# Reordered copies, transposes and output products in the attention stages of a four-layer kernel

## The chip, the cores and the metric

The kernel runs on one core of one Trainium2 chip. The metric is the device time of one execution in microseconds (us). All times below come from the runs of the kernel before the change and from one profiled execution of it.

## The reference, cut to what matters

Four layers run one after the other on one array `x` of 2048 positions by 512 channels (bf16). The first and third layers are a long convolution ("A"), the second and fourth a dilated local attention ("B"). Every layer works on a normalised copy of `x` and adds its result back:

```python
x = A_u
x = x + _A_ref(_layernorm(x), ...)      # convolution by FFT over 4096 points, per channel
x = x + _B_ref(_layernorm(x), wqkv, wo) # attention, 32 heads of 16, 8 taps at distance 2
x = x + _A_ref(_layernorm(x), ...)      # the same weights again
x = x + _B_ref(_layernorm(x), wqkv, wo)

def _B_ref(x, wqkv, wo):                # H = 32, Dh = 16, W = 8, dil = 2
    q, k, v = split_heads(x @ wqkv)
    idx = pos[:, None] - 2 * arange(8)[None, :]
    attn = softmax(where(idx >= 0, einsum(q, k[idx]) / 4, -1e9))
    return einsum(attn, v[idx]) @ wo
```

## The kernel before, in words

The kernel keeps `x` in one tile `X` of 128 partitions by 16 columns of 512 channels; `slot(m)` says which column the m-th block sits in. The change is about the two B layers. Both are built by `b_layer`; the first runs with `ln_next` (it prepares the normalisation of the A layer that follows), the second with `store` (it writes the output).

**Steps.** A B layer has N = 36 steps t. Step t takes two blocks of 114 queries out of 72 (two parities of the sequence, two halves of the heads, two quarters in each half, nine blocks). Its work on the engines is:
- `logits(t)` (L1123, PE): 16 small products of keys `KS` and queries `QS` into `S`, a PSUM tile of four banks of which there is one; then the exponential on ACT into `PT` (L1126).
- `values(t - 2)` (L1142, PE): 16 products of `PT` and `V` into the bank `O`, of which there is one; then DVE takes the reciprocal of the sums (L1146) and writes the scaled values `on` (L1150).
- two to four units of `jobs` between them: `proj` (two units of two products, L1089; DVE copies the result to a stage tile `st`, L1094, and two DMAs on the SP queue scatter its even and odd rows into `KS` or `QS`, L1097), `vproj` (one unit, L1106), and `out` (two units of two products, L1177, then the addition to `X`). `jobs` are sorted by a due step, with a first step before which they may not run: 13 for the projections of the second parity, 24 for `out`.

**Order.** On PE, DVE, ACT, POOL and SP the instructions of a B layer stand in the order in which the Python code emits them (`tc.manual_schedule`). [...]

**Late columns.** Of the 16 columns of the normalised input, the first eight are turned on PE before step 0. The other eight are made while the steps run, by `late(t)`, in two groups g = 2 and 3 of four. Each group takes four emissions, at the steps named in `steps`: statistics (DVE) and the inverse deviation (`ln_den_b`, POOL, L225 and L226); scales (DVE, L230 and L231) and four normalised columns `xq` (POOL, L260); two DMA transposes `xt<-xq` on the SP queue (L1249); four copies of the turned data into `XU` (POOL, L1255). `XU` holds the transposed input `xnT` of all projections. Its second parity needs both groups, and is first read by the projections of step 13.

**Turned values.** Every three steps the values of three steps stand in one tile `on`. `turn_o(g)` issues a DMA transpose `oS<-on` on SP (L1158) and right behind it emits the copy `oT<-oS` on POOL (L1159). It is called at t = 4, 7, 10 and so on, ahead of `late(t)` in the same step. The last two groups of three are turned on PE instead (`turn_last`, L1169, copied by DVE at L1171).

**The tail.** `out(m)` for m below 8 uses the even columns and runs inside the steps. The products of m = 8 to 15 need the last values. `ahead(m, n)` begins two of them early with n dummy products (L1326); the rest run after the last values. An odd m of the second B layer gets its residual by a product with the identity (L1199) and leaves through ACT (L1200), all others through DVE (L1195, L1202, or L236 in the tail of the first B layer). In the first B layer ACT sums the squares of the eight last columns (L241, `square`), takes two roots (L247), and DVE, POOL and ACT write the normalised columns (`unorm`, L1186 and L1183) that the A layer begins with.

**Start.** `spread` (L1080) scatters two early projections, with two SP DMAs each; `fill(n)` emits n of the statistics in the list `left` (L212). The A layer interleaves its first products `s1` with the last normalisations, which it calls as `finish[1](0)` and `finish[1](1)` (L947 and L950).

Of the kernel before, what the change touches and what calls it, by code (L numbers as in the profile page):

```python
# [816 lines left out]
def a_layer(nc, tc, C, X, kt_dram, XU, ln_b, finish):  # L817

    with ExitStack() as es:
# [123 lines left out]
        with tc.manual_schedule(engines={mybir.EngineType.PE, mybir.EngineType.DVE, mybir.EngineType.Activation}):  # L943
            s1(0, on_dve)
            finish[0]()
            s1(1, on_act)
            finish[1](0)  # L947
            warm(2)
            s1(2, split=True)
            finish[1](1)  # L950
            warm(5)
            s1(3, split=True)
            warm(3)
            zpair(0)
            turn_pe(0)
            s1(4)
            s2(0, True)
            turns(2)
            turn_pe(1, (on_act, on_act))
            ahead = {0: (5, 6), 1: (7, 8)}  # L960
            for i in range(16):
                if 0 < i < 7:
                    s2(i)
                if 6 <= i < 15:
                    s2(i + 1)
                product(i)
                if 0 < i:
                    inverse(i - 1, i > 10)
                for k in ahead.get(i, (i + 7,)):
                    if k < 16:  # L970
                        s1(k, on_dve if k == 5 else on_act)
                if i in (1, 4, 8):
                    k = i // 4 * 4 + 4
                    turns(k)
                    turns(k + 2)
                if i >= 5:
                    final(i - 5, on_dve if i in (6, 8) else on_act)
                if 10 <= i < 14:
                    ln_b.gather(X, 0, 2 * i - 20, 2 * i - 18)
            final(11)  # L980
            ln_b.gather(X, 1, 0, 3)
            inverse(15)
            ln_b.gather(X, 1, 3, 8)
            ln_b.gather(X, 0, 8, 10)
            for k in range(12, 16):
                final(k)


def b_layer(nc, tc, C, X, Wt, ln_b, XU, left, store=None, ln_next=None):

    with ExitStack() as es:
# [84 lines left out]
        def spread(k, ps, eng):  # L1076
            T, t = sets[0][1 - k // 2 % 2], stp.tile([128, 512], BF, name="st", tag="st")
            eng(t[:], ps[:])
            for e in range(2):
                nc.sync.dma_start(T[e::2, e, k // 4, UF + 512:UF + 1024], t[e::2, :])  # L1080

        def proj(n, k, eng=on_dve):

# [44 lines left out]

        ons = {}

        def values(t):
            par, fp = t // NB // 2, t // NB % 2
            pt = PT[t % 3]
            for x in range(2):
                assert (par, fp, (t % NB * 2 + x) % NB) in ready, (t, x, done)
            O = psO.tile([128, 512], F32, name="O", tag="O")[:, 0:16 * DH + 16].rearrange("p (a b) -> p a b", b=DH + 1)
            for i in range(4):
                for sl in range(4):
                    x, e = sl // 2, sl % 2
                    f2, b = (t % NB * 2 + x) // NB, (t % NB * 2 + x) % NB  # L1140
                    c0 = (i * 4 + sl) * NQ
                    nc.tensor.matmul(O[:, x * 8 + i * 2 + e, :], pt[:, c0:c0 + 128],  # L1142
                                     V[:, par * NB + b, (fp * 2 + f2) * 8 + i * 2 + e, :], start=True, stop=True,
                                     skip_group_check=True)
# [5 lines left out]
            nc.vector.tensor_tensor(on.rearrange("q (h d) -> q h d", d=DH), O[:, :, 0:DH],  # L1150
                                    rd[:].unsqueeze(2).to_broadcast([128, 16, DH]), ALU.mult)
# [4 lines left out]
        def turn_o(g):  # L1156
            oS = ld.tile([128, 6, 128], BF, name="oS", tag="oS")
            nc.sync.dma_start_transpose(oS[:], ons[g][:])  # L1158
            nc.gpsimd.tensor_copy(turned_o(g // 3, g % 3 * 3).rearrange("f (b q) -> f b q", q=NQ), oS[:, :, 0:NQ])  # L1159

        pts = {}

        def turn_last(t):
            g, s = t // 3, t % 3
# [53 lines left out]
        with tc.manual_schedule(engines={mybir.EngineType.PE, mybir.EngineType.DVE, mybir.EngineType.Activation,  # L1218
# [14 lines left out]
            def late(t):  # L1233
                if t < 4:
                    fill((len(left) + 3 - t) // (4 - t))
                for g, steps in ((2, (1, 2, 4, 6)), (3, (4, 5, 7, 9))):
                    m0 = g * 4
                    if t == steps[0]:
                        assert not [j for p, j in left if j < m0 + 4]
# [20 lines left out]
                nc.scalar.activation(ln_b.den[:, js], ln_b.mv[:, js, 1], ACT.Sqrt, bias=ln_b.eps[:, 0:1])  # L1260
            last = len(ln_b.parts) - 1
            left = list(left)
            if ln_next is not None:
                fill(3)
            ln_b.gather(X, last, 0, 4)
            ln_b.aggregate(0, 4)
            root(0)
# [5 lines left out]
            ln_b.aggregate(4, 8)  # L1273
            root(1)
            pt0 = turned(xn)
            fill(2)
            ln_b.scales(4, 8)
            xn = normed(1, (2,), (3,))
            pre = sm.tile([128, 1], F32, name="pre", tag="pre")
# [19 lines left out]
            for n in range(4):  # L1299
# [1 line left out]
                for k in ((4, 6, 5, 7) if n == 0 else (0, 2, 1, 3, 4, 6, 5, 7)):  # L1301
                    jobs.append((NB * n + k // 4 * 4 + k % 2 * 2 - 3, 2, proj(n, k), 0 if n < 2 else 13))
                jobs += [(NB * n + b // 2 + 1 + b / 100, 1, vproj(p, n % 2, b), 0 if n < 2 else 13) for b in range(NB)]
            jobs += [(N - 9 + m, 2, out(m), 24) for m in range(8)]
            jobs.sort(key=lambda j: j[0])
            due = [(d, sum(j[1] for j in jobs if j[0] <= d)) for d, *_ in jobs]
            total = due[-1][1]
# [21 lines left out]
            for t in range(N):  # L1329
                need = max([c for d, c in due if int(d) <= t] + [0])  # L1330
                end = min(total, max(need, done + ((2, 4, 4, 4, 4)[t] if t < 5 else 3)))
                if t:
                    logits(t)
                work(end - 1, t)
                if 2 <= t < N - 1:
                    values(t - 2)
                work(end, t)
                if t == N - 1:
                    assert not jobs
                    values(N - 3)  # L1340
                    ahead(8, 1)
                    turn_last(N - 4)
                    values(N - 2)
                    ahead(9, 3)
                elif t == N - 3:
                    turn_last(t - 3)
                elif t == N - 2:
                    turn_last(t - 3)
                elif t >= 4 and t % 3 == 1:
                    turn_o(t // 3 - 1)  # L1350
                late(t)
            work(total, N)
            if ln_next is not None:
                ln_next.aggregate(0, 8, C["half"])
# [1 line left out]
            values(N - 1)  # L1356
            turn_last(N - 3)
            turn_last(N - 2)
            for m in (8, 9):
                omm(tail[m], m, (2,))  # L1360
            turn_last(N - 1)
            if ln_next is not None:
                ln_next.scales(0, 8)
                for m in range(8):
                    unorm(m, nc.gpsimd)
            psS = banks("b_psL", 4)
            for m in range(10, 14):
                tail[m] = sps([128, 512])[:]
            omm(tail[10], 10, (0, 1, 2))
# [30 lines left out]
def kernel(  # L1400
# [37 lines left out]
    finish = b_layer(nc, tc, C, X, Wt, ln_b, XU, [(0, j) for j in range(12, 16)] + [x for x in late if x[0] == 1], ln_next=ln)  # L1438
# [33 lines left out]
```

## Time and profile before

| what | value |
|---|---|
| median of 7 runs | 535.7 us (531.95 to 538.41) |
| the profiled execution's own time | 535.41 us |
| its span | 533.6 us |
| mean granted PE clock | 0.936 of full speed |
| busy PE / DVE / ACT / POOL | 395.0 / 434.4 / 350.6 / 79.8 us |
| first B layer: first to last exponential | 265.50 to 352.21 us |
| second B layer: first to last exponential | 432.29 to 519.31 us |

The profile's span lies 1.8 us below the time of the same execution; what is outside it is not seen by the engines. A row of the timeline gives start, duration, engine, line, operation and, in brackets, how long the engine sat idle before it and on what. One exponential is issued per step, so the distance from one row `PT<-S` to the next is the length of a step. A row of the windows view gives the stretch, its length, the busy time of each engine, the granted PE clock, and the DMA share.

### The profile page before, as it was taken

How to read it: one execution, taken by the hardware profiler on the slowest of the kernel's cores; microseconds unless marked ns; L12 is line 12 of the kernel's file. 1: busy time of each engine (PE TensorE's matmuls, PEld its weight loads, DVE VectorE, ACT ScalarE, POOL GpSimd, SP SyncE). 2: the span in 40 equal slices, each digit the busy share in tenths (PEclk: the TensorE clock that was granted, in tenths of full speed). 3: DMA queues.
4: the chain of work that ended last, by engine and by line, in shares of the span. 5: the costliest groups of instructions: out<-in, count | busy, mean ns of one | idle time of the engine just before them, and what ended most of it. 6: DMA issues, size and time to landing. Idle time of an engine off the chain costs nothing.

```text
span 533.6 us, 15408 instructions
## 1 busy us (share of the span) xinstructions
PE 395.0 (74%) x6534; PEld 254.5 (48%) x6534; DVE 434.4 (81%) x972; ACT 350.6 (66%) x422; POOL 79.8 (15%) x129
## 2 busy tenths in 40 slices
PE   0200466487568475699898899988899788989997
PEld 0100333256246443565565465655575555646664
DVE  4999999979998997978886467887899987656663
ACT  3999834446355553544777587868888676858872
POOL 0000000000000002051137401134000214621110
PEclk9999997869688877989999799999999999989999
DMA  8301057362563247803626423317685013533542
GB/s 264 139 1 39 1 110 99 73 129 71 119 72 128 68 95 139 211 10 120 209 84 129 96 80 88 51 18 188 133 192 80 2 41 90 119 88 76 111 90 81
DMA packets 105017, 52.52 MB, mean 98 GB/s; under 512 B 86003, under 2 KB 100724, under 8 KB 103668
## 3 DMA queue, kind: packets, MB, share of 16 engines
q1 hardware_dynamic: 103364, 51.14, 41.4%
q8 instruction: 51, 0.84, 0.7%
q10 hardware_dynamic: 1584, 0.39, 0.4%
q14 instruction: 18, 0.15, 0.1%
HBM read 17.96 MB, written 8.13 MB: 49 GB/s over the span
## 4 chain that ended last, share of the span: by engine, by line
PE 33%; DVE 27%; DMA 7%; ACT 6%; issue 3%; POOL 3%; SPq 2%; ACTq 0%; DVEq 0%; POOLq 0%
PE psG L1089 6%; PE psG L1106 4%; PE O L1142 4%; PE S L1123 4%; DMA zt<-Z 3%; DVE Ytab L656 3%; DVE Y2tab L658 3%; PE psG L1177 3%; ACT PT L1126 2%; DVE ln_st_b L212 2%; DVE ta L619 2%; DVE tb L620 2%; DMA oS<-on 2%; POOL XU L1255 2%; DMA xt<-xq 1%
## 5 line engine op out<-in xcount | busy, mean ns | idle before, releaser
L1126 ACT ACTIVATE PT<-S 128x1824 bf16<-128x1824 f32 x72 | 121.8, 1691 | 42.3 <-PE S L1123 42.0
L1089 PE MATMUL psG<-XU,wqk 128*128 128x512 bf16 x224 | 65.5, 396 | 3.9 <-POOL XU L1255 3.6
L1094 DVE CAST st<-psG 128x512 bf16<-128x512 f32 x56 | 38.5, 687 | 21.8 <-PE psG L1089 20.9
L1142 PEld LDWEIGHTS <-PT 128*128 128x128 bf16 x1152 | 39.2, 96 | 18.7 <-DVE on L1150 5.8
L1142 PE MATMUL O<-V,PT 128*128 128x17 bf16 x1152 | 40.2, 171 | 3.9 <-DVE on L1150 3.5
L307 PE MATMUL psA<-X,sb_F 128*128 128x128 bf16 x128 | 13.8, 242 | 36.4 <-ACT X L720 35.2
L1106 PE MATMUL psG<-wv,XU 128*128 128x256 bf16 x288 | 40.4, 273 | 0.2 <-DVE st L1094 0.2
L307 PEld LDWEIGHTS <-sb_F 128*128 128x128 bf16 x256 | 16.2, 102 | 44.1 <-issue 41.7
L1123 PEld LDWEIGHTS <-KS 32*128 32x128 bf16 x1152 | 20.3, 94 | 28.8 <-issue 23.2
L294 ACT CAST Z<-psA 128x1024 bf16<-128x1024 f32 (+1 forms) x32 | 28.8, 984 | 7.0 <-PE psA L307 7.0
L675 PE MATMUL psk<-Ytab,Xtab 128*32 128x64 bf16 x1024 | 23.9, 206 | 12.6 <-issue 6.9
L1150 DVE TENSOR_TENSOR on<-O,rd 128x256 bf16<-128x256 f32 x72 | 30.6, 425 | 2.5
L332 PE MATMUL psA<-zt,sb_C 128*128 128x512 bf16 x30 | 15.4, 539 | 22.9 <-DMA zt<-Z 22.9
L678 PE MATMUL psk<-Y2tab,Xtab 128*32 128x48 bf16 x1024 | 23.0, 202 | 11.6 <-issue 9.5
L1123 PE MATMUL S<-QS,KS 32*128 32x114 bf16 x1152 | 28.3, 213 | 4.1 <-DMA KS<-st 1.4
L656 DVE TENSOR_TENSOR Ytab<-Ytab,MA 128x2048 bf16<-128x2048 bf16 (+1 forms) x33 | 30.7, 930 | 0.2
L658 DVE TENSOR_TENSOR Y2tab<-Ytab,MB 128x2048 bf16<-128x2048 bf16 (+1 forms) x33 | 30.7, 929 | 0.0
L1146 DVE RECIPROCAL rd<-O 128x16 f32<-128x16 f32 x72 | 18.2, 253 | 14.6 <-PE O L1142 13.1
L684 ACT CAST KTq<-psk 128x1024 bf16<-128x1024 f32 (+1 forms) x9 | 8.3, 918 | 33.2 <-issue 32.6
L1159 POOL COPY oT<-oS 128x684 bf16<-128x684 bf16 x20 | 15.1, 757 | 99.4 <-DMA oS<-on 99.4
L633 POOL MEMSET Xtab<- 128x64 bf16 x8 | 1.5, 187 | 180.6 <-PE psk L678 133.6
L678 PEld LDWEIGHTS <-Xtab 128*32 128x32 bf16 x1024 | 20.6, 101 | 16.3 <-issue 15.4
(249 smaller groups left out, 1080.9 us busy)
## 6 DMA issues: line engine op xcount, KB each, us to landing
kt_scratch<-Kt SPq DMA_DIRECT2D x4, 1024.0 KB, 3.9
Kt<-kt_scratch SPq DMA_DIRECT2D x4, 1024.0 KB, 5.5
QS<-st SPq DMA_DIRECT2D x60, 64.0 KB, 1.9
KS<-st SPq DMA_DIRECT2D x60, 64.0 KB, 1.9
X<-in_A_u_dram SPq DMA_DIRECT2D x4, 512.0 KB, 5.1
out_dram<-X SPq DMA_DIRECT2D x16, 128.0 KB, 1.8
k_scratch<-KTq SPq DMA_DIRECT2D x7, 256.0 KB, 2.4
KT<-k_scratch SPq DMA_DIRECT2D x7, 256.0 KB, 2.8
```

The lines of the kernel that those rows point to most:

```text
L294: self.nc.scalar.copy(dst, src)
L307: nc.tensor.matmul(o, F1[:, j, r, :], rhs_j(j), start=True, stop=not dk)
L656: nc.vector.tensor_tensor(v(Y[:, :, :, q * EYB:(q + 1) * EYB, :]), src, vm(self.mult(self.MA, lev, hc, EYB)), ALU.mult)
L658: nc.vector.tensor_tensor(v(Y2[:, :, :, (q - 1) * EYB:q * EYB, :]), src, vm(self.mult(self.MB, lev, hc, EYB)), ALU.mult)
L678: nc.tensor.matmul(psk[32 * g:32 * g + 32, ds, EYB:], xs, Y2[:, 1 - m // 2, h, :, t], start=False, stop=(m == 3), skip_group_check=True)
L1089: nc.tensor.matmul(ps[:], wqk[:, ct, f0:f0 + 128], xnT[:, ct, par, UF + h * 512:UF + h * 512 + 512], start=(ct == 0), stop=(ct == 3))
L1094: eng(t[:], ps[:])
L1106: nc.tensor.matmul(ps[:].rearrange("p h d -> p (h d)"), xnT[:, ct, par, NQ * b + 1:NQ * b + 1 + NK], wv[:, ct, fp * 256:fp * 256 + 256], s ...
L1123: nc.tensor.matmul(S[:, i, sl * NQ:(sl + 1) * NQ], KS[r, e, f2, b * NQ + 1:b * NQ + 1 + NK], QS[r, e, f2, UF + b * NQ:UF + b * NQ + NQ], s ...
L1126: nc.scalar.activation(pt[:, 0:16 * NQ].rearrange("k (i x) -> k i x", i=4), S[:, :, 0:4 * NQ], ACT.Exp, scale=DH ** -0.5)
L1142: nc.tensor.matmul(O[:, x * 8 + i * 2 + e, :], pt[:, c0:c0 + 128], V[:, par * NB + b, (fp * 2 + f2) * 8 + i * 2 + e, :], start=True, stop= ...
L1150: nc.vector.tensor_tensor(on.rearrange("q (h d) -> q h d", d=DH), O[:, :, 0:DH], rd[:].unsqueeze(2).to_broadcast([128, 16, DH]), ALU.mult)
```

## The change

It is one patch of seven edits:
1. `place_o` is split from `turn_o`. The transpose of group g stays at t = 3g + 4; its copy into `oT` is emitted at t = 3g + 6. `late(t)` now comes ahead of both in the step.
2. Group 3 of the late columns issues its transposes at step 6 (was 7) and its copies at step 8 (was 9).
3. `spread` issues its odd rows (e = 1) on the POOL queue, its even rows on SP.
4. Three statistics (`fill(3)`) ahead of the last gather are left out in the first B layer, and the next fill emits one instead of two; the four go to steps 0 to 3. The list `left` of that layer is sorted by group.
5. `out` jobs have due steps 28 to 33 (were 27 to 34), and from t = 32 on a step runs all its units after `values`.
6. In the last step, `values(34)` takes a bank of the `psG` pool instead of `O`, and the early start of m = 9 with its three dummies is gone. The tail takes the products in the order 8, 10, 11, 9, 12 to 15, and three of them (10, 11, 12) are begun before the last turned group is there. The first root of the squares comes after m = 12 (was 11).
7. In the A layer, the last normalisations (`finish[1](1)`) are emitted ahead of `s1(2)`.

```diff
@@ a_layer
             finish[1](0)
             warm(2)
+            finish[1](1)
             s1(2, split=True)
-            finish[1](1)
             warm(5)
@@ spread
-            for e in range(2):
-                nc.sync.dma_start(T[e::2, e, k // 4, UF + 512:UF + 1024], t[e::2, :])
+            for e, q in ((1, nc.gpsimd), (0, nc.sync)):
+                q.dma_start(T[e::2, e, k // 4, UF + 512:UF + 1024], t[e::2, :])
@@ values
-            O = psO.tile([128, 512], F32, name="O", tag="O")[:, 0:16 * DH + 16].rearrange("p (a b) -> p a b", b=DH + 1)
+            O = (gps([128, 512]) if other else psO.tile([128, 512], F32, name="O", tag="O"))[:, 0:16 * DH + 16].rearrange("p (a b) -> p a b", b=DH + 1)
@@ turn_o
             oS = ld.tile([128, 6, 128], BF, name="oS", tag="oS")
             nc.sync.dma_start_transpose(oS[:], ons[g][:])
+            oSs[g] = oS
+
+        def place_o(g):
+            oS = oSs[g]
             nc.gpsimd.tensor_copy(turned_o(g // 3, g % 3 * 3).rearrange("f (b q) -> f b q", q=NQ), oS[:, :, 0:NQ])
@@ late
-                for g, steps in ((2, (1, 2, 4, 6)), (3, (4, 5, 7, 9))):
+                for g, steps in ((2, (1, 2, 4, 6)), (3, (4, 5, 6, 8))):
@@ start of the layer
-            if ln_next is not None:
-                fill(3)
...
-            fill(2)
+            fill(1 if ln_next is not None else 2)
@@ jobs
-            jobs += [(N - 9 + m, 2, out(m), 24) for m in range(8)]
+            jobs += [((28, 29, 30, 31, 32, 33, 33.5, 33.5)[m], 2, out(m), 24) for m in range(8)]
@@ the loop over t
                 if t:
                     logits(t)
-                work(end - 1, t)
+                if t < N - 4:
+                    work(end - 1, t)
                 if 2 <= t < N - 1:
                     values(t - 2)
                 work(end, t)
+                late(t)
                 if t == N - 1:
                     assert not jobs
                     values(N - 3)
+                    values(N - 2, True)
                     ahead(8, 1)
-                    turn_last(N - 4)
-                    values(N - 2)
-                    ahead(9, 3)
-                elif t == N - 3:
-                    turn_last(t - 3)
-                elif t == N - 2:
+                if t >= N - 3:
                     turn_last(t - 3)
                 elif t >= 4 and t % 3 == 1:
                     turn_o(t // 3 - 1)
-                late(t)
+                if t >= 6 and t % 3 == 0:
+                    place_o(t // 3 - 2)
@@ the tail
-            for m in (8, 9):
-                omm(tail[m], m, (2,))
+            omm(tail[8], 8, (2,))
+            psS = banks("b_psL", 4)
+            for m in range(10, 14):
+                tail[m] = sps([128, 512])[:]
+            omm(tail[10], 10, (0, 1, 2))
+            omm(tail[11], 11, (0, 1, 2))
             turn_last(N - 1)
+            omm(tail[12], 12, (0, 1, 2))
...
-            for m in range(8, 16):
-                if m > 13:
+            for m in (8, 10, 11, 9, 12, 13, 14, 15):
+                if m == 9:
+                    tail[m] = gps([128, 512])[:]
+                elif m > 13:
                     tail[m] = sps([128, 512])[:]
-                omm(tail[m], m, (3,) if m < 11 else (0, 1, 2, 3))
+                omm(tail[m], m, (3,) if m in (8, 10, 11, 12) else (0, 1, 2, 3))
                 odone(tail[m], m)
...
-                    if m == 11:
+                    if m == 12:
                         ln_next.root_sums(8, 12)
```

More of the change, by code (lines that the diff above doesn't have):

```diff
@@ L1129, in b_layer, with values @@
         ons = {}
-        def values(t):
+        def values(t, other=False):
             par, fp = t // NB // 2, t // NB % 2
@@ L1158, in turn_o @@
             nc.sync.dma_start_transpose(oS[:], ons[g][:])
+            oSs[g] = oS
+        def place_o(g):
+            oS = oSs[g]
             nc.gpsimd.tensor_copy(turned_o(g // 3, g % 3 * 3).rearrange("f (b q) -> f b q", q=NQ), oS[:, :, 0:NQ])
-        pts = {}
+        pts, oSs = {}, {}
         def turn_last(t):
@@ L1365, in b_layer @@
                     unorm(m, nc.gpsimd)
[L1366 to L1369, printed above, removed]
-            for m in range(8, 16):
-                if m > 13:
+            for m in (8, 10, 11, 9, 12, 13, 14, 15):
+                if m == 9:
+                    tail[m] = gps([128, 512])[:]
+                elif m > 13:
                     tail[m] = sps([128, 512])[:]
-                omm(tail[m], m, (3,) if m < 11 else (0, 1, 2, 3))
+                omm(tail[m], m, (3,) if m in (8, 10, 11, 12) else (0, 1, 2, 3))
                 odone(tail[m], m)
@@ L1437 @@
     late = [(p, j) for g in (2, 3) for p in range(3) for j in range(g * 4, g * 4 + 4)]
-    finish = b_layer(nc, tc, C, X, Wt, ln_b, XU, [(0, j) for j in range(12, 16)] + [x for x in late if x[0] == 1], ln_next=ln)
+    finish = b_layer(nc, tc, C, X, Wt, ln_b, XU, sorted([(0, j) for j in range(12, 16)] + [x for x in late if x[0] == 1], key=lambda x: x[1] // 4), ln_next=ln)
     a_layer(nc, tc, C, X, kt_dram, XU, ln_b2, finish)
```

## The prediction

> **What bounds the kernel now.** The page's table of groups comes first. It shows ACT waiting for `S` between exponentials, 42 us in all over 72 steps.
>
> ```profile
> L1126 ACT ACTIVATE PT<-S 128x1824 bf16<-128x1824 f32 x72 | 121.8, 1691 | 42.3 <-PE S L1123 42.0
> ```
>
> Next the timeline, filtered to ACT, for the length of each step. There is one `S`: logits follow the exponential that frees it. A smooth step is therefore 1.69 (exponential) + 0.49 (logits) + 0.05 = 2.23 us. Three units of PE work fit beneath it (two projection units 0.86, one vproj 0.45, values 0.43, logits 0.31: 2.05); four units give 2.5 to 2.6. Three steps of the first B layer are far longer, those that begin t = 7, 13 and 14:
>
> ```profile
> 282.07 1.69 ACT L1126 ACTIVATE PT<-S 128x1824 bf16<-128x1824 f32 x1 [0.54 <-PE S L1123]
> 285.69 1.69 ACT L1126 ACTIVATE PT<-S 128x1824 bf16<-128x1824 f32 x1 [1.93 <-PE S L1123]
> ...
> 297.38 1.69 ACT L1126 ACTIVATE PT<-S 128x1824 bf16<-128x1824 f32 x1 [0.80 <-PE S L1123]
> 302.50 1.69 ACT L1126 ACTIVATE PT<-S 128x1824 bf16<-128x1824 f32 x1 [3.43 <-PE S L1123]
> 306.10 1.69 ACT L1126 ACTIVATE PT<-S 128x1824 bf16<-128x1824 f32 x1 [1.91 <-PE S L1123]
> ```
>
> They last 3.62, 5.12 and 3.60; above 2.23 that is 1.39 + 2.89 + 1.37, and step 12 (2.76) adds 0.53: 6.18 us. The second B layer has 3.70, 4.64 and 3.42: 1.47 + 2.41 + 1.19 = 5.07. Its step 1 lasts 3.47 besides.
>
> Third, the whole timeline around each, read by "who was late". At t = 7 POOL, waiting for a turned group, holds up the deviations queued behind that copy; DVE waits for these, and PE's values wait for DVE:
>
> ```profile
> 280.33 0.75 POOL L1159 COPY oT<-oS 128x684 bf16<-128x684 bf16 x1 [3.51 <-DMA oS<-on]
> 281.44 1.02 POOL L226 TENSOR_TENSOR ln_den_b<-ln_mv_b,half 128x4 bf16<-128x4 f32 x1
> 282.50 0.18 DVE L230 RECIPROCAL ln_rstd_b<-ln_den_b 128x4 f32<-128x4 bf16 x1 [2.29 <-POOL ln_den_b L226]
> 284.26 0.56 PE L1142 MATMUL O<-V,PT 128*128 128x17 bf16 x16 [1.33 <-DVE on L1150]
> ```
>
> At t = 13 SP is the cause. From 277.5 to 297 it issues almost without a break (a pair of scatters 1.2, a transpose 1.25 to 1.3). The transposes of group 3 stand late in that line, land 4.2 after issue, and the last copies of the group end when PE already waits:
>
> ```profile
> 290.21 2.63 SPq L1249 DMA_TRANSPOSE xt<-xq  x2
> 295.89 4.07 POOL L1255 COPY XU<-xt 128x512 bf16<-128x512 bf16 x4 [3.42 <-DMA xt<-xq]
> 300.02 0.59 PE L1089 MATMUL psG<-XU,wqk 128*128 128x512 bf16 x1 [0.62 <-POOL XU L1255]
> ```
>
> Fourth, the windows view (stretch, length, busy PE, PEld, DVE, ACT, POOL, PE clock, DMA share, GB/s):
>
> ```profile
> 282.00:285.40 3.40, 2.07 (x38) 0.92 (x37) 2.72 (x8) 1.69 (x1) 2.81 (x5) 1.00 0.50 127
> 297.20:300.40 3.20, 1.52 (x8) 0.40 (x5) 0.00 (x0) 1.69 (x1) 3.20 (x4) 0.83 0.43 97
> 300.40:307.80 7.40, 7.40 (x95) 3.31 (x93) 4.06 (x9) 3.38 (x2) 1.02 (x2) 0.61 0.29 73
> ```
>
> PE was 48% busy for 3.2 us, then ran at 0.50 until about 306: the stall of step 13 makes step 14 long. So these stages are bound by the copies' dates on SP and POOL, not by an engine's load.
>
> **The change part by part.** All sums are against the profiled execution, 535.41 us (span 533.6).
>
> *Edits 1 and 2, the middle of a B layer.* No instruction is added. On POOL, deviations and copies of `late` now stand ahead of `oT`; on SP, group 3's two transposes move ahead of three scatter pairs and one turned group. For the first B layer, by the trace's durations: deviations of group 3 end at 279.2 (were 282.46), DVE's L230 at 280.2 does not wait, and values run on time. The four `xq` run 280.9 to 283.9; SP then issues both transposes, 2.63, from 283.3 to 285.9. Landing takes the 3.1 to 3.3 of most transposes (288.8), at worst the 4.2 to 4.7 of group 3 before (290). POOL: group 2's copies to 288.1, first `oT` 0.8, group 3's copies 4.1: 293.0. PE needs the first at 295.7, since steps come 1.4 earlier: spare 2.7 us, or 1.5 with the worst landing. In the second B layer the spare comes out at 2.4. Queued behind the moved transposes on SP: `oS` of group 1 and the scatters of the second parity, `KS` and `QS`. Those read first land 288.5 to 289 and are needed 290.5; the next, 292.5 and 295.0. `place_o` waits for a transpose issued two steps before; its buffer (two `oS`) is copied before the third is issued. With PE never short of work, the clock has no reason to fall. Gain 6.18 + 5.07 = 11.25 at most. What is late next: three statistics in steps 0 to 2 and two in step 3 (before 2, 2, 2 and 1), each 0.24 to 0.35 on a DVE that is full there, +0.2; not every step comes down to 2.23, +0.7. I take −10.35.
>
> Here a page speaks against a part of that sum. The Trainium skill, "TensorE: Matmul & The Clock Gate", section "HAM oscillation", has the clock fall after idle gaps over some 3.4 us. No gap on PE here exceeds 0.7 us between 297 and 300.4, and it fell all the same. By the rule the low clock in step 14 isn't the stall's work and 1.37 + 1.19 stay; the sum would be −7.8. The row decides: in both B layers the clock falls right behind this stall, and at 282.0 to 285.4 (61% busy) it held.
>
> *Edit 4, start of the first B layer.*
>
> ```profile
> 242.48 2.86 DVE L212 BATCH_NORM_STATS2 ln_st_b<-X 128x6 f32<-128x384 bf16 x6
> 245.25 0.68 DVE L477 CAST Kt<-psA 128x512 bf16<-128x512 f32 x1
> 248.84 0.28 PE L405 MATMUL psA<-sb_IC,y 128*128 128x256 bf16 x1 [0.55 <-DVE y L398]
> ```
>
> The cast's product was ready at about 244.4; three statistics (half of 2.86, 1.4) go from ahead of it, and the casts and gathers behind are 1.1 to 1.35 earlier up to the last one at 253.4, PE waiting for DVE throughout. Part is spent on waiting for PE: −1.1, bounds −1.4 and −0.6. One fewer in `fill`: −0.1, which lies beside waits, so nothing is booked. Cost of their new place: counted above.
>
> *Edit 3, `spread` on POOL.* The trace of before has no DMA from POOL. In the second B layer, logits of t = 2 waited for a scatter:
>
> ```profile
> 437.39 0.50 PE L1123 MATMUL S<-QS,KS 32*128 32x114 bf16 x16 [1.13 <-DMA KS<-st]
> ```
>
> It was issued at 433.8 and took 3.5; others of SP 1.8 to 2.4. Two issues of 0.55 leave SP for an idle POOL. Best case: the 1.28 of that step; worst, later than now. The Trainium skill, "DMA: Bandwidth & Descriptors", speaks against it: in "Issuing engines are not separate DMA queues" a second issuer saves only issue time; and "Anatomy of one DMA — SWDGE (gpsimd) path" gives 2.0 us + bytes/436e3, for 64 KB an estimate of 2.15. By row: issue 0.55 earlier, landing 1.9. By rule: 0.25 later per half, so 0.3 gained. The late half was an even one, still on SP, so only the earlier issue helps: −0.4, bounds −1.28 and + several us (the last rival). 2.42 us lie between cast and need.
>
> *Edits 5 to 7, the ends.* Steps 30 and 31 fall from 2.61 to 2.23, step 33 becomes values 0.56 + 12 output products 2.6 + turn 0.4 = 3.55 (was 2.69 and 2.32): +0.10 for the first B layer, +0.47 for the second. In the second, `values(34)` in another bank starts about 1 us earlier after the last exponential, and 24 products of 0.2155 instead of 27 follow the last turn, −0.65: net −0.2. In the first, DVE and ACT set the end. Values of t = 33 wait behind L236 and statistics on DVE, and the deviations for POOL's `unorm` come later, +0.26. The first root (361.62) follows five squares instead of four, 0.72 more each: DVE's L255 waits 0.77 with all behind it. `finish[1](1)` ahead of `s1(2)` puts an `XU` on ACT ahead of evacuations that PE's L855 needs: in sum +1.0 at L876, which begins at 369.30. I book +1.1 (bounds 0 and +2). The new bank hides nothing here, so this part loses.
>
> **Sum.** −10.35 − 1.1 − 0.4 − 0.2 + 1.1 = −10.95: 535.41 becomes 524.4. The median of the runs (535.7) lies 0.3 above the profiled execution: 524.7 us.
>
> **The rivals.**
> *Half of it comes back (19%).* Scatters behind the moved transposes land late, at t = 11 or 13, or the copies of group 3 still end late because transposes take 4.7 while SP is full; the stall shrinks, and the clock still falls. For: SP has no slack in that stretch, and total issues are the same. Against: the spare of 1.5 to 2.7. Half of 11.25 stays: about 529.5 (527 to 532).
> *It does not do what it says in the tail.* Product order and the extra bank cannot shorten the first B layer's end while ACT has eight squares of 0.72 and roots; already in my sum. If PE, 49% busy for 3.4 us at t = 34 by my times, also drops to half clock, +1.0 to +1.7: 526, inside the range of the first case.
> *No change (6%).* New dates on SP produce the same stall at another step: 533 to 538.
> *Slower (8%), one mechanism.* POOL's scatters land late, and logits(2) wait in each B layer: everything runs on `S`, so the wait is paid in full, and PE, idle, then runs at half clock, about 1.4 as at step 14. Without edit 3's gain the rest gives −10.55. A wait w costs 2(w + 1.4); with w = 3.9 it is even with before, from w = 5.2 on (landing 7.7 after the cast, 2.42 being free) it is slower by over 0.5%. At w = 8: −10.55 + 18.8, 543.7 + 0.3 = 544. For: nothing shows POOL's queue. Against: the slowest scatter read above took 3.5.
>
> **How the numbers follow.** About 0.5% (2.7 us: 533.0 to 538.4) is what a measurement here can tell from no change. Likeliest case 67%: 524.7, own range 521 to 527; half back 19%; no change 6%; slower 8%. Faster is 67 + 19 = 86%. The range 520.5 to 531 holds the first case and most of the second, and leaves out both others.
>
> **What would show it right or wrong.** Right: steps 7, 13 and 14 at 2.2 to 2.4 in both layers; group 3's transposes issued at 283 to 286, its copies ended before PE asks; PE's clock at 1.00 for the ten us behind step 13; step 33 at about 3.5; the first exponential 1.1 earlier; L876 of the next layer about 1.1 later, measured from the last exponential. Wrong: PE waiting for `KS`, `QS` or `XU` between t = 9 and 15; a wait over 2 us for `KS` at t = 1 or 2; POOL's own queue busy during `spread`; the low clock in step 14 without a stall ahead of it.

## The result, and the profile after

The changed kernel takes 529.9 us (median of 22 runs, 526.39 to 533.55) where the kernel before takes 535.2 (57 runs): a ratio of 0.9912, 95% interval 0.9893 to 0.9931. By this ratio it is faster by 4.7 us (3.7 to 5.7), clear of noise, but by less than half of the 11 us forecast; 529.9 lies inside the stated range of 520.5 to 531.0, but far from 524.7. The profiled execution has a span of 528.9 us, 4.7 below that of before.

Medians are of all executions, ratios leave out those more than 1.5% above the fastest of their kernel, and the only profiles of `a_spread_sp`, `a_order` and `a_both_root` are of such executions, so that their spans are not used.

In the page's table of groups ACT still waits for `S`, 38.0 us instead of 42.0:

```profile
L1126 ACT ACTIVATE PT<-S 128x1824 bf16<-128x1824 f32 x72 | 121.8, 1691 | 38.5 <-PE S L1123 38.0
```

The timeline of the changed kernel (the lines from L1159 to L1262 of before are four higher here) shows the middle of the first B layer repaired. POOL works in the order of emission: before, the deviations of group 3 ran at 281.44, behind a copy that had waited 3.51 us. Now they end at 278.5 and DVE no longer waits for them; the transposes of group 3 are issued at 284.7 and its copies end at 293.5.

```profile
277.45 1.02 POOL L226 TENSOR_TENSOR ln_den_b<-ln_mv_b,half 128x4 bf16<-128x4 f32 x1
279.39 0.17 DVE L230 RECIPROCAL ln_rstd_b<-ln_den_b 128x4 f32<-128x4 bf16 x1
...
284.69 2.65 SPq L1253 DMA_TRANSPOSE xt<-xq  x2
289.34 4.14 POOL L1259 COPY XU<-xt 128x512 bf16<-128x512 bf16 x4 [1.69 <-DMA xt<-xq]
...
295.50 1.69 ACT L1126 ACTIVATE PT<-S 128x1824 bf16<-128x1824 f32 x1 [0.92 <-PE S L1123]
297.73 1.69 ACT L1126 ACTIVATE PT<-S 128x1824 bf16<-128x1824 f32 x1 [0.54 <-PE S L1123]
300.36 1.69 ACT L1126 ACTIVATE PT<-S 128x1824 bf16<-128x1824 f32 x1 [0.94 <-PE S L1123]
```

Step 13 lasts 2.23 (was 5.12) and step 14 lasts 2.63 (was 3.60). At the layer's end the same view shows what was lost; these are the ACT and PE rows of steps 32 to 34:

```profile
338.57 1.69 ACT L1126 ACTIVATE PT<-S 128x1824 bf16<-128x1824 f32 x1
339.27 0.57 PE L1142 MATMUL O<-V,PT 128*128 128x17 bf16 x16 [0.81 <-DVE on L1150]
...
341.62 1.69 ACT L1126 ACTIVATE PT<-S 128x1824 bf16<-128x1824 f32 x1 [1.36 <-PE S L1123]
342.60 0.55 PE L1142 MATMUL O<-V,PT 128*128 128x17 bf16 x16 [1.09 <-DVE V L1108]
343.00 2.79 PE L1181 MATMUL psG<-wo_t,oT 128*128 128x512 bf16 x12
345.63 0.27 PE L1173 MATMUL psG<-sb_ident,on 114*128 114x114 bf16 x2
345.83 0.38 PE L1123 MATMUL S<-QS,KS 32*128 32x114 bf16 x16
346.32 1.69 ACT L1126 ACTIVATE PT<-S 128x1824 bf16<-128x1824 f32 x1 [3.01 <-PE S L1123]
```

Values come first in their step now. PE therefore reaches them 0.8 and 1.1 us before it can run them (bank `O` is not free, a cast of `V` is late on DVE), and everything behind waits too: in step 33 twelve products, the turn and the next logits. Before, four products stood ahead of the values in step 33, and PE then waited 0.22 us for the cast of `V`:

```profile
347.12 1.08 PE L1177 MATMUL psG<-wo_t,oT 128*128 128x512 bf16 x4
348.42 0.55 PE L1142 MATMUL O<-V,PT 128*128 128x17 bf16 x16 [0.22 <-DVE V L1108]
```

PE was busy for 2.04 of 2.60 us in step 34 before (windows view, columns as in the prediction's fourth view):

```profile
350.01:352.61 2.60, 2.04 (x53) 1.68 (x54) 1.87 (x5) 2.06 (x2) 0.37 (x1) 1.00 0.00 0
```

Steps 32 and 33 last 3.05 and 4.70 (were 2.23 and 2.69). Step 34 is left nearly empty of PE work, and the same view shows the price:

```profile
346.35:348.95 2.60, 0.97 (x37) 0.73 (x34) 2.36 (x5) 2.06 (x2) 0.00 (x0) 1.00 0.00 0
350.05:353.55 3.50, 3.50 (x30) 1.99 (x29) 2.32 (x14) 1.68 (x3) 1.12 (x2) 0.54 0.02 7
363.05:366.55 3.50, 3.28 (x16) 1.51 (x15) 1.90 (x7) 2.74 (x5) 0.00 (x0) 0.56 0.92 382
```

PE was busy 0.97 of 2.60 us (2.04 before); then its clock ran at half for 3.4 us, and once more from 14.9 us behind the last exponential on, again for 3.4 us. Before, the clock was 1.00 from step 34 to the end of this tail.

The difference of the two spans, cut at the exponentials (us, minus is faster):

| stretch | forecast | measured |
|---|---|---|
| start to the first exponential (edit 4) | -1.1 | -1.31 |
| step 1 of both layers (edit 3) | -0.4 | +0.58 and +0.25 = +0.83 |
| steps 2 to 29 of both layers (edits 1 and 2) | -10.35 | -5.00 and -4.32 = -9.32 |
| steps 30 to 33 of both layers (edit 5) | +0.57 | +2.07 and +1.00 = +3.07 |
| last exponential of the first B layer to the first of the second (edits 6 and 7) | +1.0 | +1.98 |
| end of the second B layer (edit 6) | -0.65 | +0.01 |
| sum | -10.93 | -4.74 |

The middle came close. The steps' end and what follows it took 5.1 us where the forecast had 0.9.

### The profile page after: what moved, and what is told of

It is laid out like the page before. It is cut to its first block, busy times and chain, and to the rows that moved or that the text cites. A ratio compares the mean times of both kernels' runs of the same rounds, so it can differ in the third digit from the quotient of the medians.

```text
span 528.9 us, 15391 instructions
## 1 busy us (share of the span) xinstructions
PE 392.4 (74%) x6528; PEld 256.2 (48%) x6528; DVE 432.9 (82%) x972; ACT 350.3 (66%) x422; POOL 83.0 (16%) x133
## 4 chain that ended last, share of the span: by engine, by line
PE 33%; DVE 28%; ACT 8%; DMA 6%; issue 4%; SPq 1%; POOL 0%; ACTq 0%; DVEq 0%
PE psG L1089 5%; PE psG L1106 4%; ACT PT L1126 4%; PE S L1123 4%; PE O L1142 3%; PE psG L1181 3%; DVE Ytab L656 3%; DVE Y2tab L658 3%; DMA zt<-Z 3%; DMA KS<-st 2%; DVE ta L619 2%; DVE tb L620 2%; DVE ln_st_b L212 2%; DVE pa L898 1%; PE S L1181 1%
## 5 line engine op out<-in xcount | busy, mean ns | idle before, releaser
L1089 PE MATMUL psG<-XU,wqk 128*128 128x512 bf16 x224 | 61.4, 380 | 0.4 <-DVE V L1108 0.4
L1142 PE MATMUL O<-V,PT 128*128 128x17 bf16 x1120 | 38.9, 171 | 2.9 <-DVE V L1108 1.5
L1106 PEld LDWEIGHTS <-XU 128*128 128x128 bf16 x288 | 25.4, 98 | 7.3 <-issue 0.2
L1146 DVE RECIPROCAL rd<-O 128x16 f32<-128x16 f32 x70 | 17.7, 253 | 13.4 <-PE O L1142 11.7
```

The costliest lines, as they stand in the source:

```text
L1089: nc.tensor.matmul(ps[:], wqk[:, ct, f0:f0 + 128], xnT[:, ct, par, UF + h * 512:UF + h * 512 + 512], start=(ct == 0), stop=(ct == 3))
L1106: nc.tensor.matmul(ps[:].rearrange("p h d -> p (h d)"), xnT[:, ct, par, NQ * b + 1:NQ * b + 1 + NK], wv[:, ct, fp * 256:fp * 256 + 256], s ...
```

## The experiments

Every kernel is timed beside the kernel before on its chip. With intervals of 0.4 to 0.7% either way, times tell apart the large parts only; for one edit the step lengths of the profile decide, and those that the program sets repeat to 0.1 us.

**Edits 1 and 2 alone (`mid_only`, and again as `mid_again`).**

```diff
 (the kernel before)
-                for g, steps in ((2, (1, 2, 4, 6)), (3, (4, 5, 7, 9))):
+                for g, steps in ((2, (1, 2, 4, 6)), (3, (4, 5, 6, 8))):
-                late(t)          # behind turn_o
+                late(t)          # ahead of turn_o
+                if t >= 6 and t % 3 == 0:
+                    place_o(t // 3 - 2)
```

> The kernel before with edits 1 and 2 alone: place_o split off behind late, group 3 turned and copied one step sooner. Theory (the middle of the B layers gives what the prediction booked, nearly): steps 7, 13 and 14 at 2.2 to 2.6 in both layers, steps 5 to 29 together 9 to 10 us less, no loss elsewhere: about 526 us beside 535.5. Rival (part of the gain needs the other edits, or is given back in the A layer between): 529 or more, with steps 13 or 14 still over 3 us.

> The kernel with edits 1 and 2 alone once more, with more rounds: how much of the step lengths repeats. Theory (steps 7, 13, 14 and 30 to 33 are set by the program, steps 1, 10 and 11 by pauses of SP's queue that fall differently in each execution): steps 7, 13, 14, 30 to 33 agree with the first run to 0.1 us; steps 1, 10 and 11 need not. Time about 525, 0.98 of before. Rival (the step lengths of 1, 10 and 11 belong to the kernel): all of them repeat.

Measured: 524.28 us, ratio 0.9802 (0.9738 to 0.9866); again 526.44, ratio 0.9847 (0.9803 to 0.9890). Steps 7, 13 and 14 are 2.23 to 2.26 in both layers of both runs. The first profile has a span of 521.9, 11.7 below before: from first to last exponential the two layers gain 5.5 and 6.4 us, of which 1.3 is a shorter step 1 of the second, which is no work of these edits. So two of the seven edits beat all seven together, and the loss must be sought in edits 3 to 7.

**Edit 1 alone (`mid_edit1`).** As `mid_only`, with the steps of group 3 left at `(4, 5, 7, 9)`.

> The kernel before with edit 1 alone: place_o split off and behind late, the transposes and copies of group 3 still at steps 7 and 9. Theory (edit 1 frees the deviations from the copy of the turned values, edit 2 brings group 3 forward): step 7 falls to 2.23 in both layers; since the transposes now stand ahead of the turned group of step 7, and steps are earlier, group 3 lands sooner than before but one step later than with edit 2: of the 8.2 us of steps 13 and 14 between a quarter and a half stay, and the clock still falls in step 14. Rival (edit 1 alone brings the whole gain): steps 13 and 14 at 2.3 or less; rival (edit 1 gives step 7 alone): step 13 near 5 in the first layer.

Measured: 530.48 us, ratio 0.990 (0.9867 to 0.9934). Step 7 is 2.23 in both layers; steps 13 and 14 are 3.64 and 2.23 in the first, 4.31 and 2.99 in the second (before: 5.12 and 3.60, 4.64 and 3.42). The timeline gives the reason: transposes issued at 290.1, copies at 296.1, over five us after POOL was free.

```profile
290.09 2.64 SPq L1253 DMA_TRANSPOSE xt<-xq  x2
292.79 1.30 SPq L1158 DMA_TRANSPOSE oS<-on  x1
296.11 4.10 POOL L1259 COPY XU<-xt 128x512 bf16<-128x512 bf16 x4 [5.36 <-DMA xt<-xq]
```

Edit 1 alone cures step 7 and a part of step 13; the rest needs edit 2, as the theory had it. Of the 7.9 us that steps 13 and 14 of both layers had above 2.23, 4.2 stay, a little more than the half that was expected at most. The clock fell in the second layer alone: in the first, step 14 stayed at 2.23 behind a step 13 of 3.64 (the last section has the figures).

**The units ahead of the values again (`a_order`), and the old due steps (`a_dates`).** Each undoes half of edit 5 in the changed kernel.

```diff
 (a_order)
-                if t < N - 4:
-                    work(end - 1, t)
+                work(end - 1, t)
 (a_dates)
-            jobs += [((28, 29, 30, 31, 32, 33, 33.5, 33.5)[m], 2, out(m), 24) for m in range(8)]
+            jobs += [(N - 9 + m, 2, out(m), 24) for m in range(8)]
```

> The changed kernel, but from step 32 on the units run ahead of the values again, all but the last (the output products keep their new due steps). Theory (values that are emitted first wait on PE for the bank O and for DVE's cast of V, and all units stand behind them): step 32 of the first B layer falls from 3.05 to about 2.3, step 33 from 4.70 to about 3.5; in the second B layer step 33 from 3.98 to about 3.5. Together some 2.5 us less. Rival (the due steps, which put twelve products into step 33, make it long by themselves, and the order does nothing): step 33 stays over 4. The low clock behind step 34 of the first B layer should remain if a thin step 34 causes it, and go if the stall in step 33 does.

> The changed kernel with the due steps of the output products of before (27 to 34), with the units behind the values from step 32 on as changed. Theory: steps 30 and 31 return to 2.6, step 33 of the first B layer falls from 4.70 to some 3.1 (the waits of the values, 1.1 us, stay, the eight extra products go), step 34 has work again, so that PE's clock no longer falls behind it, and the first addition of the tail comes about 1 us sooner after the last exponential. Rival (the order alone makes step 33 long): step 33 stays over 4 and the clock falls as before.

Measured: 529.47 us, ratio 0.9888 (0.9847 to 0.9929), and 527.28, ratio 0.9866 (0.9801 to 0.9932). Steps in us, first layer / second layer:

| kernel | 30 and 31 | 32 | 33 | first addition, after the last exponential |
|---|---|---|---|---|
| before | 2.61 / 2.61 | 2.23 / 2.23 | 2.69 / 2.32 | 5.71 |
| changed | 2.23 / 2.23 | 3.05 / 2.33 | 4.70 / 3.98 | 6.85 |
| a_order | 2.23 / 2.23 | 2.23 / 2.23 | 3.61 / 3.60 | 6.89 |
| a_dates | 2.61 / 2.61 | 3.09 / 2.38 | 3.40 / 2.68 | 5.24 |

Both halves cost: the order some 0.8 in step 32 and 1.1 in step 33 of the first layer (the two waits above), the dates 0.9 to 1.3 in step 33, where six products more stand (12 instead of 6), against 0.8 that they save in steps 30 and 31. With the order undone, steps 30 to 33 of both layers together are 0.68 us longer than before, where the forecast for them was 0.57. `a_dates` came out a little off its expectation: step 33 at 3.40 (3.1 was expected), the first addition 1.6 us sooner (1). And the dates alone decide over the clock: `a_order` still has an empty step 34 and a low clock behind it, `a_dates` has neither. Its PE is busy 1.72 of the same 2.60 us, and that suffices:

```profile
348.04:350.64 2.60, 1.72 (x56) 1.47 (x54) 2.37 (x5) 2.06 (x2) 0.00 (x0) 1.00 0.00 0
351.74:355.24 3.50, 3.32 (x35) 2.21 (x34) 2.52 (x14) 1.68 (x3) 1.84 (x2) 1.00 0.03 7
```

**Step 34 filled with dummies (`a_pad34`).** The changed kernel, with one line that computes nothing:

```diff
+                if t == N - 2:
+                    warm(8)
                 if 2 <= t < N - 1:
                     values(t - 2)
```

> The changed kernel with eight dummy products (272 columns each, into the bank O) ahead of the values of step 34, and nothing else. Theory (PE's clock falls behind step 34 because that step leaves PE 0.97 us of work in 2.60): PE's clock stays at 1.00 in the five us behind the last exponential of the first B layer, the first addition of its tail comes 5.7 to 5.9 us after that exponential where it came after 6.85, steps 32 and 33 are unchanged at 3.05 and 4.70. Rival (the order of the tail's products makes the addition late): it stays at 6.6 or more with the clock at 1.00. Open: whether the second low clock, 14.5 to 18 us behind, goes with the first.

Measured, by the windows view in the same places as for the changed kernel:

```profile
349.08:351.68 2.60, 2.05 (x47) 1.53 (x46) 2.35 (x5) 2.06 (x2) 0.00 (x0) 1.00 0.00 0
352.78:356.28 3.50, 3.36 (x36) 2.26 (x34) 2.59 (x15) 1.67 (x3) 1.63 (x2) 1.00 0.01 2
365.78:369.28 3.50, 3.37 (x33) 2.03 (x32) 2.12 (x5) 2.88 (x7) 0.00 (x0) 1.00 0.60 253
```

Both low clocks are gone. The first addition comes at 5.68 (was 6.85), the turn of `Z` (L876) at 16.87 (was 19.27), the next layer's first exponential 79.64 after the last (was 82.05). Eight useless products win 2.41 us, while steps 32 and 33 stay at 3.05 and 4.70: it is the empty step, not the long one, that costs the clock. The other profiles agree: from the last exponential to the next layer's first it takes 81.6 to 82.1 us in the three kernels whose step 34 is empty (the changed one, `a_order`, `a_spread_sp`), 79.1 to 80.1 in the other eleven. The time of the whole, 529.87 us and a ratio of 0.990 (0.9862 to 0.9937), can't show it; this execution began its first B layer 3 us later than that of the changed kernel, which the edit doesn't touch.

**Edit 5 undone as a whole (`a_both`), and then the root behind four squares (`a_both_root`, `root_again`).** Both diffs of edit 5 above, and for the latter two

```diff
-                    if m == 12:
+                    if m == 9:
                         ln_next.root_sums(8, 12)
```

> The changed kernel with its fifth edit undone as a whole: output products due in steps 27 to 34, units ahead of the values in all steps. Theory (the fifth edit alone turned the end of the steps into a loss, and edits 4, 6 and 7 gain a little): steps 30 to 33 as before the change (2.61, 2.61, 2.23, 2.69; second layer 2.62, 2.60, 2.23, 2.32), first addition 5.2 after the last exponential, the next layer's turn of Z at 16.4, the second B layer's end at 13.7: a span about 1 to 3 us below that of the kernel with edits 1 and 2 alone (521.9), some 520, the luck of the scatters of steps 1 and 10 aside. Rival (the new tail order costs as predicted, +1.1 us): no better than 523.

> The same with the first root of the squares behind four squares (after m = 9 in the new order) where the change put it behind five. Theory (of the prediction: the fifth square delays the root and all that DVE has behind it): the first root comes 3.6 instead of 4.3 us after the first addition, and the turn of Z up to 0.7 us earlier than in the run without it. Rival (ACT is not what the end of this stage waits for): the root moves, the turn of Z does not.

> The changed kernel without edit 5 and with the root behind four squares, once more. Theory (long steps 10 and 11 in its first profile were such pauses): they come out shorter than 5.1 and 4.8, or in another layer; the tail repeats (first root 9.2, turn of Z 16.4, end 13.9). Its time is 1 to 3 us below that of edits 1 and 2 alone, which the intervals may not tell apart. Rival (steps 10 and 11 of about 5 belong to this kernel): they repeat, and it is slower than edits 1 and 2 alone.

Measured: `a_both` 523.25 us, ratio 0.9797 (0.9735 to 0.9859). Steps 30 to 33 are back at 2.61, 2.61, 2.23, 2.70; first addition 5.49, turn of `Z` 16.68, end of the second layer 13.97. Against the changed kernel's profile that is 3.06 in the steps, 2.60 in the tail and 0.37 at the end: edit 5 costs 6.0 us, and the two ratios, 1.15 points apart, say the same. The part of the run's expectation that put its span 1 to 3 us below that of `mid_only` did not come true (522.1 against 521.9). With the root behind four squares: 525.14, ratio 0.9781 (0.9705 to 0.9858), and again 523.75, ratio 0.9803 (0.9754 to 0.9853). ACT and DVE rows of the tail, first of `a_both`, then of `root_again`, whose last exponentials lie at 346.92 and 346.64:

```profile
356.69 0.29 ACT L247 ACTIVATE ln_den_a<-ln_st_a,eps 128x4 bf16<-128x4 f32 x1
357.01 0.18 DVE L255 RECIPROCAL ln_rstd_a<-ln_den_a 128x4 f32<-128x4 bf16 x1 [0.84 <-ACT ln_den_a L247]
```

```profile
355.83 0.30 ACT L247 ACTIVATE ln_den_a<-ln_st_a,eps 128x4 bf16<-128x4 f32 x1
356.16 0.18 DVE L255 RECIPROCAL ln_rstd_a<-ln_den_a 128x4 f32<-128x4 bf16 x1 [0.28 <-ACT ln_den_a L247]
```

DVE's wait falls from 0.84 to 0.28, but the turn of `Z` comes only 0.30 sooner (16.38). The end of the second layer takes 13.9 to 14.0 in these kernels, 14.3 to 14.8 in those without edits 6 and 7. With 520.8, `root_again` has the shortest span of all. In time it is below both the kernel before and the changed one; from `mid_only` the intervals don't part it.

**The early scatters (`a_spread_sp`, `mid_pool`).** Edit 3 taken out of the changed kernel, and edit 3 added to `mid_only`:

```diff
 (a_spread_sp; mid_pool the other way round)
-            for e, q in ((1, nc.gpsimd), (0, nc.sync)):
-                q.dma_start(T[e::2, e, k // 4, UF + 512:UF + 1024], t[e::2, :])
+            for e in range(2):
+                nc.sync.dma_start(T[e::2, e, k // 4, UF + 512:UF + 1024], t[e::2, :])
```

> The changed kernel with its third edit undone: both halves of the two early scatters go out on SP again. Theory (a scatter issued by POOL lands in 2.8 to 3.1 us where SP's take 1.9, so the keys of step 2 come later): step 1 of the first B layer returns from 2.76 to about 2.2 us, that of the second from 3.73 to at most 3.5; the POOL queue disappears from the table of DMA queues; about 0.8 us less than the changed kernel in all. Rival (the three statistics moved into steps 0 to 2 hold up DVE's casts and so the keys): step 1 of the first B layer stays at about 2.7.

> The kernel with edits 1 and 2 alone, plus edit 3: the odd halves of the two early scatters on POOL's queue. Theory (POOL's scatter takes longer to land than SP's, but what makes step 1 long is a pause of SP's own queue that hits by chance): step 1 is 2.2 to 2.8 in a layer without a pause of SP in the scatters that follow, over 3 with one, as without edit 3; the time is that of edits 1 and 2 alone within 2 us. Rival (edit 3 helps, as predicted, 0.4 us or more): step 1 at 2.2 in both layers, also where SP pauses; rival (edit 3 is a loss): over 2.7 in both layers.

Measured: 531.07 us, ratio 0.9915 (0.9876 to 0.9955), and 525.42, ratio 0.9843 (0.9784 to 0.9902). Step 1 is 3.83 and 3.17 without edit 3, 2.18 and 2.17 with it alone: the opposite of what the pair of profiles above suggested. What step 1 follows is a pause of SP, seen in its own rows of the changed kernel:

```profile
430.73 0.49 SPq L1080 DMA_DIRECT2D QS<-st  x1
432.12 0.47 SPq L1080 DMA_DIRECT2D KS<-st  x1
432.99 2.02 SPq L1097 DMA_DIRECT2D QS<-st  x2
```

The issue of that pair takes 1.10 to 1.19 as a rule; here it took 2.02, and the keys that went out just ahead landed 3.7 us after their issue, on SP's queue and on POOL's alike. The 14 profiles hold 28 beginnings of a B layer. In all nine where this pair took 1.35 to 2.42, step 1 is 3.17 to 3.83; in the other 19 it is 2.17 to 2.24, but for the 2.76 of the changed kernel's first layer. Pauses fell in 3 of 16 beginnings with edit 3 and in 6 of 12 without; the mean of step 1 is 2.46 and 2.82. That leans towards edit 3, and is too little to settle it. (The last section shows what the pauses go with.)

**The two transposes taken apart (`b_split`).** A try for a better version: `a_both_root` without edit 3, and one transpose of group 3 at step 6, one at step 7.

```diff
-                    elif t == steps[2]:
+                    elif t == steps[2] or (g == 3 and t == steps[2] + 1):
...
-                        for h in range(2):
+                        for h in ((0, 1) if g == 2 else (t - steps[2],)):
```

> The changed kernel with edits 3 and 5 undone and the root behind four squares, and with the two transposes of group 3 taken apart: one at step 6, one at step 7, so that the scatters of step 7 stand between them on SP. Theory (steps 10 and 11 grow when a pause of SP hits the scatters that stand behind two transposes in a row): steps 10 and 11 at 2.2 to 2.5 in both layers even then; group 3 lands about 1.3 later, which the spare of 2 us holds. Rival (the spare is not there): step 13 grows to 3 or more as copies of group 3 end late. About 520 to 523 us if the theory holds.

Measured: 526.54 us, ratio 0.985 (0.9793 to 0.9907), no gain to be seen; the rival came true. Steps 10 and 11 are 2.23, but step 13 is 3.30 and 3.63, since PE is at the projections before the copies are:

```profile
296.76 0.38 PE L1089 MATMUL psG<-XU,wqk 128*128 128x512 bf16 x1 [0.24 <-POOL XU L1261]
297.76 0.38 PE L1089 MATMUL psG<-XU,wqk 128*128 128x512 bf16 x1 [0.62 <-POOL XU L1261]
```

The spare ahead of step 13 is thus smaller than the delay of a split transpose. Steps 10 and 11 of 5.1 and 3.3 us in the profile of `a_both_root` were the reason for this version; `root_again`, the same kernel, has 2.23 there, and nothing is built on them.

## Why the prediction was right or wrong

- **The middle (edits 1 and 2): right.** -9.32 against -10.35 in the first pair of profiles, and `mid_only` gives the whole forecast by itself. The places and the order of dates hold: transposes forecast for 283.3 and found at 284.7, the end of the copies forecast for 293.0 and found at 293.5. The nearness of these dates is in part luck, since the layer began 1.3 us sooner: counted from its first exponential, the transposes came 2.7 us later than forecast and the copies ended 1.8 later. The spare ahead of PE's first reading product was 1.8 us in both layers, not 2.7 and 2.4. `mid_edit1` confirms that edit 1 frees step 7 and edit 2 is needed for step 13. What the changed kernel lacks of it is mostly in steps 10 to 14 (0.1 to 0.7 each), single waits for scatters that `mid_only` does not have in the same places.
- **The start (edit 4): right in kind, less in size.** Between DVE's `y` that PE waits for at 241.80 (before) or 241.41 (changed) and the first exponential lie 23.69 to 23.70 us in the five profiles without edit 4 and 22.76 to 23.26 in the nine with it, 22.77 in the changed kernel's: -0.93, within the stated bounds. The other 0.4 lies ahead of it, where the same code differs by up to 3 us between executions.
- **Step 33 (edits 5 to 7): the first step that failed.** The sum of its work, "values 0.56 + 12 output products 2.6 + turn 0.4 = 3.55", is what PE does there. But I let values begin with the step. They began 1.0 us after it, behind DVE's cast of `V` (PE had waited 1.09 us), and step 32, which I left at 2.23, had such a wait of its own (0.81). `a_order` confirms it: with the units ahead of the values again, step 33 is 3.61. So the failed term is the wait of the values, which I put at nothing: I did not ask what covers it when no units stand ahead of the values any more. Steps 30 to 33 cost 2.5 us more than booked in both layers together (3.07 against 0.57).
- **The tail of the first layer: +1.98 instead of +1.0, and for another reason, so that the sign is luck.** The forecast's reasons, the root behind five squares and the order of `finish[1](1)`, do not add up to a loss: with edit 5 undone, edits 6 and 7 make the turn of `Z` 0.44 earlier than in `mid_only`, and the root is worth 0.30, not 0.77. The loss is the low clock behind an empty step 34. I had it as an aside under the rivals ("+1.0 to +1.7") and at nothing in the sum; `a_pad34` puts it at 2.4. It belonged into the sum: the row that said that PE at 48% loses its clock was already in the text, and step 34 was forecast at 49% of 3.4 us (found: 52%).
- **The second layer's end: -0.65 was right for edit 6** (13.9 to 14.0 with it and without edit 5, 14.3 to 14.8 without both), and +0.01 in the changed kernel's profile. Its last cast begins 0.8 sooner after the last exponential (10.25 instead of 11.07), but the span closes 0.8 later behind it. That last part stays open.
- **Edit 3: not settled.** The -0.4 was read from one late scatter, and +0.83 is what one pair of profiles shows; both are mostly the luck of SP's pauses. POOL's landing, the price that I bounded, took 1.9 to 3.7 us in the 32 scatters of the eight profiles that have them. The two halves of one scatter, one on each queue, landed within 0.5 us of each other's time every time, so the late ones (3.69 on POOL, 3.72 on SP) show no cost of POOL's queue. The estimate of 2.15 from the Trainium skill ("DMA: Bandwidth & Descriptors", "Anatomy of one DMA — SWDGE (gpsimd) path") and SP's 1.9 that I took both lie in that range; neither foresaw the 3.7.
- **The clock.** The prediction set the row against the Trainium skill's rule of idle gaps ("TensorE: Matmul & The Clock Gate", "HAM oscillation"). In the changed kernel's step 34 the longest wait of PE is 1.24 us, and the clock fell; filling the step kept it up. The measurement decides: what went with the falls here is a low share of busy time, not a long gap.

So the mechanism forecast for the gain was right, and the loss lay in the edit that I had taken for a small rearrangement. Edit 5 cost 6.0 us where 0.6 was booked; that explains nearly all of the miss of 6.2.

## What to carry to other kernels

- When you move an instruction that depends on others ahead of independent work on an engine that works in order, ask what it waits for, the bank that it writes included; the work that stood there was the cover, and all that follows inherits the wait.
- Treat the evenness of PE's load as a resource. Emptying a step and overfilling its neighbour can cost as much in clock as in order (here 2.4 us each); a few dummy products, or two real ones left in place, show it at once.
- When several edits come together, run the one with the mechanism by itself; and read a term from step lengths that repeat over executions, since one pair of profiles puts chance waits down to an edit.

## What was not expected of the hardware

- PE's clock changes on a fixed grid of time. In all 14 profiles it is either 1.00 or 0.50, and each value lasts a whole multiple of 3.41 us (but for the last one, which the trace cuts off). Cut at these dates, the changed kernel's two falls look alike:

```profile
346.42:349.84 3.42, 1.79 (x63) 1.51 (x60) 2.66 (x7) 2.88 (x2) 0.00 (x0) 1.00 0.00 0
349.84:353.25 3.41, 3.41 (x29) 1.95 (x28) 2.53 (x14) 1.89 (x3) 0.82 (x2) 0.50 0.02 7
360.08:363.49 3.41, 1.76 (x14) 0.88 (x12) 3.38 (x9) 2.77 (x8) 2.78 (x4) 1.00 0.78 279
363.49:366.90 3.41, 3.37 (x17) 1.73 (x16) 1.46 (x6) 2.30 (x4) 0.00 (x0) 0.50 0.81 336
```

  PE was busy 52% of the stretch ahead of each. In `a_pad34` the stretch with step 34 has 84% and the sparsest one behind it 71% (2.43 us), and the clock held. In `mid_edit1` the stretch ahead of step 14 has 65% in the first layer, where it held, and 58% in the second, where it fell. From 230 us on, all falls stand behind stretches of 64% or less; behind some of 49 to 64% it held, and what decides there is open. Where a sparse step lies in this grid is chance: in the second layer of the changed kernel step 34 falls into two stretches of 75% and 83%, and the clock held.
- SP's pauses go with packets of instructions. A pair of scatters takes 1.1 to 1.2 us to issue; every 5.4 to 9.5 us of the changed kernel's B layers a pause hits one (it then takes 1.35 to 2.4 in the beginnings counted above), and transfers issued just ahead land 3.2 to 3.8 us after issue instead of 1.9. The DMA view of the long pair at 432.99 (queue, packets, MB, share) has a row of another kind:

```profile
q8 instruction: 1, 0.02, 4.3%
```

  This is one packet of 16 KB. In the 14 profiles 159 scatters of SP took over 0.75 us to issue, and 153 of them overlap such a packet; of the 1489 shorter ones 152 do. That the packet makes the pause is not shown by an experiment. What sets its date stays open: in the two profiles of the kernel with edits 1 and 2 alone, step 1 of the first layer is 2.18 and 3.38.
